# Attention and two feed-forward layers on one core: new costs and ranks in the planner that orders all work, and two small jobs moved to GpSimd

## The chip, the cores and the metric

The kernel runs on 1 core of a Trainium2 chip. The metric is device time in microseconds (us) of one execution; the time before is the median of 3 runs, 767.08 us (765.8 to 771.89).

## The reference

Three stages follow each other. Everything is float32 (the weights of the two feed-forward layers arrive as float64 words and are decoded on the chip).

- Attention: 16 heads (2 batches of 8), 768 positions, 64 channels. Six sign bits per position (q or k times a 64x6 matrix, compared with 0) give a bucket number; a query sees only keys of its own bucket. Scores are scaled by 1/8, softmax has a guard of 1e-9 in its sum, and the result is multiplied with v.
- First layer on 1536 tokens: `h = (x @ w1) * (x @ w2)`, then `h @ w3 @ w_out` (512 to 1024 to 1024 to 512 channels).
- Second layer: `silu(x @ w_gate) * (x @ w_val) @ w_out` (512 to 1536 to 512 channels).

## The kernel before

**Arithmetic.** Most float32 products are split into a rounded high part and a low part, and one product is three matmuls (`split_mm`, L284 to L286: high by high, high by low, low by high).

**Attention.** A tile `s` is 128 queries of one head against all 768 keys; there are 96 tiles, six per head. Each tile passes: scores `S{s}` on TensorE (L626, L627); `clip{s}` on VectorE, which copies the scores with a floor and takes their maximum; `nm{s}` on VectorE (the maximum times -0.125); `exp{s}` on ScalarE (L646), which also gives the row sums; six transposes `T{s}` on TensorE (L655); the two evacuations of those, `h1_{s}` on ScalarE (L659, high part) and `h2_{s}` on VectorE (low part). Two tiles make a group: `av{n}a` and `av{n}b` on TensorE (L724, L725), `ev{n}` on ScalarE (L734, L735), then `add`, `mul` and `xlo` on GpSimd. After a head's last tile its row sums get the guard and the reciprocal (`rs{hh}` on VectorE) and go to all partitions through two transfers (`so`, `si`).

**Loading a head.** `head(hh)` for heads 2 to 15 loads raw q and k (`ldraw`, SyncE's queue), loads them once more with rounding (`cast1`, two transfers issued by GpSimd, tile `KQ`, since the source is float32 and the target a rounded type), copies parts of `KQ` on the chip (`cast2` and `cast3`, SyncE's queue, tiles `KH` and `QL`), subtracts for the low parts (`lok`, `loq`, on VectorE or GpSimd), computes the bucket bits (`proj` on TensorE, `bits` on VectorE) and moves 12 rows of bits (`rows`, SyncE's queue, L569). Only then can the first score tile of the head run. There are two sets of head buffers, so a head's loads wait for the last score tile of the head before the previous one.

**Weights.** A `piece` of weights (128x512) is loaded by SyncE's queue, decoded in four steps (`e`: exponent and leading bits, `l`: next bits, on ScalarE; `s`: sign word; `b`: the bits put together on VectorE) and split in a high part `h` and a low part `r`. Step `s` may run on ScalarE or GpSimd, whichever the planner picks, and so may `e`. 24 pieces (w3, w_out) serve the product `WP` of these two matrices, whose 192 matmuls fill TensorE between attention tiles; 16 pieces (w1, w2) serve the first layer for 512 tokens ("f" products, while attention ends); 36 pieces serve the second layer for these tokens ("m" and "acc"). From about 458 us on the other 1024 tokens run through both layers with fewer products (`pair(1, ...)`, `pair(2, ...)`); the set of inputs of `pair(1, ...)`, tiles `X1...`, is prepared by `xset` before.

**The planner.** All this is written as operations with alternatives (engine and assumed cost), inputs, resources and a rank (`prio`, lower goes first). `Plan.run` steps a clock: on each engine that is free it starts the ready operation of lowest rank. The order it finds is the order in which instructions are issued; on the chip each engine and each queue goes through its own list in that order and waits in front of an instruction whose input is late. For a transfer the planner assumes a single channel (`dma_free`), a time in it (`xfer`), 0.65 and 0.9 us around it and an extra `wait`; `queue` is how many us the channel may be booked ahead for an operation to start (`Q_LOAD` for weights and v, `Q_HEAD` for heads). An operation that may not run on GpSimd and VectorE together declares a `port`; GpSimd operations of that kind wait for the VectorE ones before them.

The ranks before, as far as they matter: heads `P_HEAD` -2.6; `nm` and `rs` -1 plus 0.001 per tile; decoding and splitting of w1 and w2 `P_DF` -1, of the second layer's weights and the layers' own evacuations `P_DEC` -1; `X1` preparation `P_T` -1; evacuations `P_EV` -0.9; products with v and their evacuation `P_AV` -0.5; `exp` 0; `clip` `P_CLIP` 0.2; w3 and w_out `P_DW` 0.45. On TensorE a product of `WP` number m ranks as tile `W_FROM` + `W_STEP` m. `W_GATE` and `F_GATE` place weight loads behind score tiles, and `N_GATE` holds the `X1` preparation back until the loads of that stage of the second layer have landed.

Of the kernel before, what the change touches and what calls it, by code (L numbers as in the profile page):

```python
# [15 lines left out]
ALU = mybir.AluOpType  # L16
# [14 lines left out]
N_R, N_SUM = 1, 2  # L31
N_DEC_MOE, N_SA_MOE, N_OT = 1, 0, 2
N_ST = 5
P_OUT, P_SPLIT, P_T, P_X2, N_GATE = -3, -2, -1, -2, 4
N_WARM = 20
W_GATE, F_GATE = (2, 1), (24, 0.8)
Q_LOAD, Q_HEAD = 6, 8
P_TPE = -1
X_W, WP_W = 3, 4
PEN = 0.05  # L40
S_POOL = 0
P_DEC, P_DW, P_DF = -1, 0.45, -1
P_CLIP, P_EV, P_AV, P_HEAD = 0.2, -0.9, -0.5, -2.6
W_FROM, W_STEP = 24, 0.75
LO_ALT, LO_FAST = 1, 4
MARGIN = (2, 0)


# [1 line left out]
BOTH = ("POOL", "DVE")  # L50
# [6 lines left out]
class Plan:  # L57
# [1 line left out]


    LAT = {
        ("PE", "PE"): 0.0, ("PE", "ACT"): 0.2, ("PE", "DVE"): 0.2, ("ACT", "PE"): 0.32, ("DVE", "PE"): 0.31,
        ("POOL", "PE"): 0.31, ("SP", "PE"): 0.3, ("DVE", "POOL"): 0.2, ("ACT", "POOL"): 0.17, ("POOL", "DVE"): 0.08,
        ("POOL", "ACT"): 0.1,
    }
# [5 lines left out]
    def op(self, name, alts, deps=(), prio=0.0, acq=(), rel=(), wait=0.0, xfer=0.0, after=(), queue=1e9, port=("POOL",)):  # L71
        o = Op()
        o.name, o.alts, o.deps, o.prio, o.acq, o.rel = name, alts, [d for d in deps if d is not None], prio, acq, rel
        o.seq, o.users, o.seen, o.end, o.wait, o.xfer = len(self.ops), [], [], None, wait, xfer
        o.after = [d for d in after if d is not None]
        o.nexts, o.queue, o.port = [], queue, port
        self.ops.append(o)
        return o
# [109 lines left out]
def moe_after_bucket_attention(ctx: ExitStack, tc: tile.TileContext, qk, vv, pp, cst, w12, w3t, w_out, wgv, wo2, out):  # L188
    nc = tc.nc
    PE, ACT, DVE, POOL, SP = nc.tensor, nc.scalar, Kept(nc.vector), Kept(nc.gpsimd), nc.sync  # L190
# [34 lines left out]
    env = {}  # L225
# [73 lines left out]
    op = plan.op  # L299
# [174 lines left out]
    def head(hh):  # L474
        i = hh % 2
        a, q, k = KQ[i], QL[i], KH[i]
        before = sc.get(6 * (hh - 1) - 1)
# [94 lines left out]
        if hh < 2:  # L572
            z = 0.3 * hh
            l1 = op(f"first{hh}k", [("SP", 1.1, load_part(1))], [], -22 + hh, xfer=1.0, acq=[("W", 1)])
            o0 = o1 = op(f"first{hh}q", [("SP", 1.1, load_part(0))], [], -21.5 + hh, xfer=1.0, acq=[("W", 1)])
            r1 = op(f"round{hh}k", [("ACT", c_act(S), lambda: round_part(1))], [l1], pr_ - 3 + z)
            c3 = [("POOL", c_pool_mul(S), copy3(POOL)), ("ACT", c_act(S), copy3(ACT))]
            oc = op(f"cast3_{hh}", c3[hh : hh + 1], [l1], pr_ - (1 if hh else 6) + z)
            r0 = op(f"round{hh}q", [("ACT", c_act(S), lambda: round_part(0))], [o0], pr_ - 2.5 + z)
            o2 = op(f"cast2_{hh}", [("ACT", c_act(S), copy2)], [r1], pr_ - 2 + 2 * z)  # L580
            o3 = op(f"lok{hh}", [("DVE", c_dve(S), lo_k(DVE))], [r1, oc], pr_ + z, rel=[("W", 1)], port=BOTH)
            o4 = op(f"loq{hh}", [("DVE", c_dve(S), lo_q(DVE))], [r0, o3], pr_ - 1 + z, rel=[("W", 1)], port=BOTH)
        else:
            o0 = op(f"ldraw{hh}", [("SP", 1.1, load)], [before], pr_ - 2, acq=[("raw", 1)], xfer=1.4, queue=Q_HEAD)
            ok = o1 = op(f"cast1_{hh}", [("POOL", 2.35, cast1)], [before], pr_ - 2, xfer=2.8, queue=Q_HEAD, wait=1.0, port=())
            o2 = op(f"cast2_{hh}", [("SP", 0.48, cast2)], [before, ok], pr_ - 2, xfer=0.75, after=[o1])
            oc = op(f"cast3_{hh}", [("SP", 0.48, cast3)], [before, o1], pr_ - 2.1, xfer=0.75, after=[o1])
            o3 = op(f"lok{hh}", lo_alts(lo_k), [o0, ok], pr_, port=BOTH)
            o4 = op(f"loq{hh}", lo_alts(lo_q), [o0, o1, o3], pr_, rel=[("raw", 1)], port=BOTH)
# [27 lines left out]
    def tile_ops(s):  # L617
        hh, qt = divmod(s, 6)
        i, n, kk = hh % 2, s // 2, s % 2
        a, q, k = KQ[i], QL[i], KH[i]  # L620
        qs = slice(qt * 128, qt * 128 + 128)

        def scores():
            ps = two(f"S{s}")
            for c0, c1 in ((0, 512), (512, S)):
                PE.matmul(ps[:, c0:c1], a[:, 0, qs], a[:, 1, c0:c1], start=True, stop=False)  # L626
                PE.matmul(ps[:, c0:c1], q[:, qs], k[:, c0:c1], start=False, stop=True)  # L627

        def clip():
            env[f"ms{s}"] = ap.tile([128, S], F32, tag="ms", name=f"ms{s}", bufs=N_MS)  # L630
            env[f"mx{s}"] = ap.tile([128, 2], F32, tag="mx", name=f"mx{s}", bufs=6)
            ps = end_two(f"S{s}")
            DVE.tensor_scalar(
                out=env[f"ms{s}"], in0=ps[:, 0:S], scalar1=-BIG, scalar2=None, op0=ALU.max, op1=ALU.max,
                accum_out=env[f"mx{s}"][:, 0:1],
            )

        def negmax():
            m = env[f"mx{s}"]
            DVE.tensor_scalar(out=m[:, 1:2], in0=m[:, 0:1], scalar1=-0.125, scalar2=None, op0=ALU.mult)  # L640

        def expo():
            m, p = env.pop(f"mx{s}"), env[f"ms{s}"]
            if qt == 0:
                env[f"sums{hh}"] = ap.tile([128, 6], F32, tag="sums", name=f"sums{hh}", bufs=N_SUM)
            ACT.activation(p, p, AF.Exp, bias=m[:, 1:2], scale=0.125, accum_out=env[f"sums{hh}"][:, qt : qt + 1])  # L646

        def open_p():
            if kk == 0:
                env[f"P{n}"] = ap.tile([128, 2, 12, 128], F32R, tag="P", name=f"P{n}", bufs=N_PT)  # L650

        def pe_transp():
            ps, p = two(f"T{s}"), env.pop(f"ms{s}")
            for c in range(6):
                PE.transpose(ps[:, c * 128 : c * 128 + 128], p[:, c * 128 : c * 128 + 128], ident)  # L655

        def pe_first():
            open_p()
            ACT.copy(env[f"P{n}"][:, kk, 0:6], env[f"T{s}"][:, 0:S].rearrange("p (c q) -> p c q", c=6))  # L659

        def pe_second():
            v = end_two(f"T{s}")[:, 0:S].rearrange("p (c q) -> p c q", c=6)
            p = env[f"P{n}"][:, kk]
            sub(DVE, p[:, 6:12], v, f(p[:, 0:6]))

        pr_ = P_ATT + s * 0.001
        deps = [sc.get(s - 1), lo_op.get(s - N_MS - 1)]
        if qt == 0:
            deps += head_ready[hh]
        sc[s] = op(f"S{s}", [("PE", c_pe(4, 384), scores)], deps, pr_, acq=[("two", 1)])  # L670
        o1 = op(f"clip{s}", [("DVE", c_dve(S) + 0.12, clip)], [sc[s], clip_prev[0]], pr_ + P_CLIP, acq=[("ms", 1)], rel=[("two", 1)])
        clip_prev[0] = o1
        o2 = op(f"nm{s}", [("DVE", 0.07, negmax)], [o1], pr_ - 1)
        o3 = op(f"exp{s}", [("ACT", 0.93, expo)], [o2, exp_op.get(s - 1)], pr_, acq=[("sums", 1)] if qt == 0 else [])
        acq_p = [("PT", 1)] if kk == 0 else []
        opened = p_open.get(n)
        o6 = op(f"T{s}", [("PE", 0.58, pe_transp)], [o3, setup_ld], pr_ + P_TPE, acq=[("two", 1)], rel=[("ms", 1)])
        lo_op[s] = o6
        o6 = op(f"h1_{s}", [("ACT", c_act(S) - 0.08, pe_first)], [o6], pr_ + P_EV, acq=acq_p, after=[opened])
        p_open[n] = o6  # L680
        t_op[s] = op(f"h2_{s}", [("DVE", c_dve(S), pe_second)], [o6], pr_ + P_EV, rel=[("two", 1)])
        exp_op[s] = o3
        if qt == 5:
            rowsums(hh, o3, pr_)

    def rowsums(hh, last, pr_):

        e = hh % 2

        def recip():  # L690
            sm = env[f"sums{hh}"]
            DVE.tensor_scalar(out=sm, in0=sm, scalar1=1e-9, scalar2=None, op0=ALU.add)
            DVE.reciprocal(sm, sm)

        def put():
            env[f"rd{hh}"] = dpool.tile([128, 6], F32, name=f"rd{hh}")
            SP.dma_start(out=env[f"rd{hh}"], in_=env.pop(f"sums{hh}"))

        def get():
            if e == 0:  # L700
                env[f"R{hh // 2}"] = ap.tile([128, S], F32, tag="R", name=f"R{hh // 2}", bufs=N_R)
            row = env.pop(f"rd{hh}").rearrange("p c -> (p c)").partition_broadcast(64)
            SP.dma_start(out=env[f"R{hh // 2}"][64 * e : 64 * e + 64], in_=row)

        o1 = op(f"rs{hh}", [("DVE", 0.31, recip)], [last], pr_ - 1, port=BOTH)
        o2 = op(f"so{hh}", [("SP", 0.55, put)], [o1], pr_ - 3, xfer=0.05, wait=0.4, rel=[("sums", 1)])
        r_op[hh] = op(f"si{hh}", [("SP", 0.55, get)], [o2], pr_ - 3, xfer=0.15, wait=0.4, acq=[("R", 1)] if e == 0 else [])

# [976 lines left out]
```

## Time and profile before

| | before |
|---|---|
| median of 3 runs | 767.08 us |
| the profiled execution | 766.29 us, its span 764.5 us |
| TensorE busy | 742.8 us (97%) |
| VectorE busy | 541.1 us (71%) |
| ScalarE busy | 463.5 us (61%) |
| GpSimd busy | 320.5 us (42%) |
| TensorE clock granted | full speed in all 40 slices |
| DMA, 16 engines | 50.4% (hardware queues), 6.5% (software queue) |

The span runs from the first to the last instruction. Busy time is the union of an engine's instructions; a matmul's end is modelled, so consecutive matmuls overlap in the record (one is shown with 0.39 us where the next begins 0.23 us later). "Idle before <- releaser" names what ended the pause in front of an instruction.

### The profile page before, as it was taken

The page shows a single profiled execution, that of the slowest core. Times are in us where ns is not written, and L with a number is a line of the kernel's source. Part 1 is how long each engine was busy: PE and PEld are TensorE (multiplying, and loading weights), DVE is VectorE, ACT ScalarE, POOL GpSimd, SP SyncE. Part 2 cuts the span into 40 slices and gives each one's busy share as a digit, 9 for nine tenths or more (in the row PEclk, how much of TensorE's full clock was granted, in tenths as well). Part 3 has the DMA queues.
Part 4 walks back from the last instruction along what each step waited for, and adds up shares of the span by engine and source line. Part 5 has one row for each costly group of instructions (what it writes and reads, how often), then busy time and mean ns, then how long its engine had stood idle before and what let it go on. Part 6 is the DMA issues. An engine that isn't in the chain of part 4 may idle for free.

```text
span 764.5 us, 11354 instructions
## 1 busy us (share of the span) xinstructions
PE 742.8 (97%) x3888; PEld 627.1 (82%) x3888; DVE 541.1 (71%) x957; ACT 463.5 (61%) x835; POOL 320.5 (42%) x338
## 2 busy tenths in 40 slices
PE   8989999999999989999999999999999999999997
PEld 5867798888999868888788888888888888888886
DVE  7879897888878878556798555667676774555550
ACT  6979988999878979786897753212244322331200
POOL 3566758576545746534311234523401645330000
PEclk9999999999999999999999999999999999999999
DMA  8875566665569794599877975221225433455011
GB/s 268 216 184 140 132 170 155 163 161 135 143 153 256 218 280 150 173 353 350 286 276 281 364 269 202 101 84 55 83 73 165 139 120 110 165 167 191 28 56 55
DMA packets 43329, 135.10 MB, mean 177 GB/s; under 512 B 7893, under 2 KB 10069, under 8 KB 43273
## 3 DMA queue, kind: packets, MB, share of 16 engines
q1 hardware_dynamic: 41032, 123.38, 50.4%
q0 software_dynamic: 2240, 11.01, 6.5%
q8 instruction: 31, 0.51, 0.3%
q14 instruction: 26, 0.20, 0.1%
HBM read 97.85 MB, written 30.46 MB: 168 GB/s over the span
## 4 chain that ended last, share of the span: by engine, by line
PE 77%; DMA 8%; ACT 6%; POOL 3%; DVE 3%; issue 2%; SPq 0%; POOLq 0%; ACTq 0%; DVEq 0%
DMA KQ<-in_qk_dram 5%; PE T L655 4%; PE pacc_two L286 3%; PE pacc_two L284 3%; PE pacc_two L285 3%; PE m L284 3%; PE av L724 3%; PE m L285 3%; PE m L286 3%; PE av L725 3%; PE a L284 2%; PE a L286 2%; PE a L285 2%; PE c L286 2%; PE c L284 2%
## 5 line engine op out<-in xcount | busy, mean ns | idle before, releaser
L181 DVE TENSOR_SCALAR_CACHE_REDUCE ms<-S 128x768 f32<-128x768 f32 x96 | 91.4, 952 | 21.8 <-PE S L627 15.7
L181 DVE TENSOR_TENSOR P<-T,P 128x768 fp32r<-128x768 f32 x96 | 90.5, 952 | 10.2 <-ACT P L659 9.4
L646 ACT ACTIVATE ms<-ms,mx 128x768 f32<-128x768 f32 x96 | 89.8, 936 | 10.8 <-DVE mx L181 10.1
L655 PE MATMUL T<-cs,ms 128*128 128x128 f32 x576 | 78.3, 273 | 7.0 <-ACT ms L646 3.1
L659 ACT CAST P<-T 128x768 fp32r<-128x768 f32 x96 | 75.5, 794 | 9.3 <-PE T L655 6.2
L655 PEld LDWEIGHTS T<-cs,ms 128*128 128x128 f32 x576 | 65.4, 140 | 14.3 <-ACT ms L646 5.5
L724 PE MATMUL av<-P,VP 128*128 128x256 f32 x288 | 74.2, 292 | 0.9 <-ACT tt L735 0.7
L725 PE MATMUL av<-P,VP 128*128 128x256 f32 x288 | 71.5, 283 | 0.7 <-DVE P L181 0.7
L626 PE MATMUL S<-KQ 128*128 128x512 f32 x192 | 67.2, 353 | 4.2 <-DVE ms L181 2.1
L627 PE MATMUL S<-KH,QL 128*128 128x512 f32 x192 | 60.7, 339 | 2.2 <-DMA KH<-QL 1.5
L724 PEld LDWEIGHTS av<-P,VP 128*128 128x128 f32 x288 | 54.6, 190 | 3.3 <-ACT tt L735 2.8
L725 PEld LDWEIGHTS av<-P,VP 128*128 128x128 f32 x288 | 54.8, 190 | 1.3 <-DVE P L181 0.9
L626 PEld LDWEIGHTS S<-KQ 128*128 128x128 f32 x192 | 36.2, 188 | 13.2 <-DVE ms L181 3.7
L1392 ACT COPY u<-a 128x512 f32<-128x512 f32 x20 | 11.7, 587 | 55.5 <-PE a L286 55.4
L181 POOL TENSOR_TENSOR sl_F<-sl_F 128x256 f32<-128x256 f32 x30 | 22.2, 738 | 53.0 <-DVE sl_F L181 41.6
L627 PEld LDWEIGHTS S<-KH,QL 128*128 128x128 f32 x192 | 36.2, 189 | 8.7 <-DMA KH<-QL 1.6
L290 ACT ACTIVATE dec_w2x<-sl_raww2x 128x512 f16<-128x512 f32 (+1 forms) x54 | 39.0, 734 | 2.8 <-DVE sl_raww2x L181 2.1
L284 PE MATMUL m<-sl_X,sl_w2x 128*128 128x512 f32 x96 | 37.5, 391 | 1.0 <-ACT sa_m L937 1.0
L286 PE MATMUL m<-sl_X,sl_w2x 128*128 128x512 f32 x96 | 37.4, 390 | 0.0
L285 PE MATMUL m<-sl_X,sl_w2x 128*128 128x512 f32 x96 | 37.4, 390 | 0.0
L181 POOL TENSOR_TENSOR KQ<-kqraw,KQ 64x768 fp32r<-64x768 f32 x11 | 20.3, 1849 | 27.4 <-DVE ms L181 8.1
L181 DVE SCALAR_TENSOR_TENSOR sl_raww2x<-dec_w2x,dec_w2x 128x512 uint32<-128x512 uint32 x36 | 25.8, 721 | 7.7 <-ACT dec_w2x L290 5.4
(302 smaller groups left out, 2194.9 us busy)
## 6 DMA issues: line engine op xcount, KB each, us to landing
dram<-sl_w2x SPq DMA_DIRECT2D x36, 512.0 KB
sl_raww2x<-in_wgv_dram SPq DMA_DIRECT2D x24, 512.0 KB
KQ<-in_qk_dram POOLq DMA_DIRECT2D x28, 384.0 KB, 6.1
sl_wA<-dram SPq DMA_DIRECT2D x20, 512.0 KB
sl_wB<-dram SPq DMA_DIRECT2D x20, 512.0 KB
sl_raww<-in_w3t_dram SPq DMA_DIRECT2D x16, 512.0 KB
sl_raww12f<-in_w_dram SPq DMA_DIRECT2D x16, 512.0 KB
dram<-sl_w12f SPq DMA_DIRECT2D x16, 512.0 KB
```

Of the source, the lines that this page charges most:

```text
L181: self.got.append(call(*a, **k))
L284: PE.matmul(ps, a_hi, b_hi, start=first, stop=False, skip_group_check=more)
L285: PE.matmul(ps, a_hi, b_lo, start=False, stop=False, skip_group_check=more)
L286: PE.matmul(ps, a_lo, b_hi, start=False, stop=last, skip_group_check=more)
L290: ACT.activation(out_, in_, AF.Copy, scale=by)
L626: PE.matmul(ps[:, c0:c1], a[:, 0, qs], a[:, 1, c0:c1], start=True, stop=False)
L627: PE.matmul(ps[:, c0:c1], q[:, qs], k[:, c0:c1], start=False, stop=True)
L646: ACT.activation(p, p, AF.Exp, bias=m[:, 1:2], scale=0.125, accum_out=env[f"sums{hh}"][:, qt : qt + 1])
L655: PE.transpose(ps[:, c * 128 : c * 128 + 128], p[:, c * 128 : c * 128 + 128], ident)
L659: ACT.copy(env[f"P{n}"][:, kk, 0:6], env[f"T{s}"][:, 0:S].rearrange("p (c q) -> p c q", c=6))
L724: PE.matmul(ps[:, 0:256], vab, p[:, :, c], start=c == 0, stop=False)
L725: PE.matmul(ps[:, 0:256], vab, p[:, :, 6 + c], start=False, stop=c == 5)
```

## The change

It edits constants of the planner, two of its latencies, the assumed cost of the rounding load, and the row sums' code. The rounding load is taken to occupy GpSimd for 1.12 us instead of 2.35 and to be usable 4.2 us after the modelled transfer instead of 1.0. Evacuations rank at -2.6 instead of -0.9, heads at -4.5 instead of -2.6, `clip` at 0.7 instead of 0.2. Sign words list GpSimd before ScalarE (`S_POOL`). Heads 2 to 4 list GpSimd before VectorE for their subtractions (`LO_FAST` from 4 to 1). The guard of the row sums becomes an operation of its own on GpSimd, and only the reciprocal stays on VectorE. The two latencies into TensorE grow from 0.32 and 0.31 to 0.37 and 0.36.

```diff
-P_OUT, P_SPLIT, P_T, P_X2, N_GATE = -3, -2, -1, -2, 4
+P_OUT, P_SPLIT, P_T, P_X2, N_GATE = -3, -2, 1, -2, 6
-W_GATE, F_GATE = (2, 1), (24, 0.8)
-Q_LOAD, Q_HEAD = 6, 8
+W_GATE, F_GATE = (2, 2), (37, 1.8)
+Q_LOAD, Q_HEAD = 8, 5
-S_POOL = 0
-P_DEC, P_DW, P_DF = -1, 0.45, -1
-P_CLIP, P_EV, P_AV, P_HEAD = 0.2, -0.9, -0.5, -2.6
-W_FROM, W_STEP = 24, 0.75
-LO_ALT, LO_FAST = 1, 4
+S_POOL = 1
+P_DEC, P_DW, P_DF = -1.5, 2.15, -0.7
+P_CLIP, P_EV, P_AV, P_HEAD = 0.7, -2.6, -0.65, -4.5
+W_FROM, W_STEP = 10, 1
+LO_ALT, LO_FAST = 1, 1
+CAST_WAIT = 3
...
-        ("PE", "PE"): 0.0, ("PE", "ACT"): 0.2, ("PE", "DVE"): 0.2, ("ACT", "PE"): 0.32, ("DVE", "PE"): 0.31,
+        ("PE", "PE"): 0.0, ("PE", "ACT"): 0.2, ("PE", "DVE"): 0.2, ("ACT", "PE"): 0.37, ("DVE", "PE"): 0.36,
...
-            ok = o1 = op(f"cast1_{hh}", [("POOL", 2.35, cast1)], [before], pr_ - 2, xfer=2.8, queue=Q_HEAD, wait=1.0, port=())
+            ok = o1 = op(f"cast1_{hh}", [("POOL", 1.12, cast1)], [before], pr_ - 2, xfer=2.8, queue=Q_HEAD, wait=CAST_WAIT + 1.2, port=())
...
-        o2 = op(f"nm{s}", [("DVE", 0.07, negmax)], [o1], pr_ - 1)
+        o2 = op(f"nm{s}", [("DVE", 0.07, negmax)], [o1], pr_ - 1, port=())
...
+        def guard():
+            sm = env[f"sums{hh}"]
+            POOL.tensor_scalar(out=sm, in0=sm, scalar1=1e-9, scalar2=1.0, op0=ALU.add, op1=ALU.mult)
+
         def recip():
-            sm = env[f"sums{hh}"]
-            DVE.tensor_scalar(out=sm, in0=sm, scalar1=1e-9, scalar2=None, op0=ALU.add)
-            DVE.reciprocal(sm, sm)
+            DVE.reciprocal(env[f"sums{hh}"], env[f"sums{hh}"])
...
-        o1 = op(f"rs{hh}", [("DVE", 0.31, recip)], [last], pr_ - 1, port=BOTH)
+        last = op(f"rp{hh}", [("POOL", 0.15, guard)], [last], pr_ - 1)
+        o1 = op(f"rs{hh}", [("DVE", 0.14, recip)], [last], pr_ - 1, port=())
```

## Rows read from the trace of the kernel before

**Rows 1.** Windows over the whole span: length, busy us (count) by engine, clock, DMA share, GB/s

```profile
0.00:20.00 20.00, 15.86 (x65) 11.69 (x66) 15.40 (x32) 14.10 (x22) 7.32 (x13) 1.00 0.88 270
20.00:100.00 80.00, 72.07 (x494) 62.65 (x493) 69.07 (x139) 73.24 (x142) 52.90 (x58) 1.00 0.70 169
100.00:260.00 160.00, 159.62 (x1047) 142.60 (x1046) 133.41 (x262) 140.88 (x267) 101.15 (x105) 1.00 0.67 172
260.00:320.00 60.00, 55.69 (x359) 47.68 (x357) 47.02 (x87) 51.77 (x99) 32.98 (x37) 1.00 0.59 187
320.00:380.00 60.00, 58.87 (x259) 48.10 (x258) 36.61 (x54) 45.27 (x75) 26.23 (x29) 1.00 0.91 326
380.00:760.00 380.00, 380.00 (x1674) 314.15 (x1673) 238.84 (x387) 137.68 (x234) 99.93 (x96) 1.00 0.43 149
760.00:764.50 4.50, 0.65 (x3) 0.19 (x2) 0.71 (x2) 0.59 (x1) 0.00 (x0) 0.96 0.61 233
```

**Rows 2.** TensorE's timeline: four of its longest waits between 40 and 300 us

```profile
48.72 0.50 PE L627 MATMUL S<-KH,QL 128*128 128x512 f32 x1 [1.31 <-DMA KH<-QL]
58.25 0.47 PE L626 MATMUL S<-KQ 128*128 128x512 f32 x1 [0.89 <-DVE P L181]
91.76 0.84 PE L655 MATMUL T<-cs,ms 128*128 128x128 f32 x6 [1.21 <-DVE QL L181]
284.12 0.88 PE L655 MATMUL T<-cs,ms 128*128 128x128 f32 x6 [2.58 <-ACT ms L646]
```

**Rows 3.** The chain that ended last (start us, us, what): rounding loads in it

```profile
23.03 11.12 DMA KQ<-in_qk_dram
60.45 5.33 DMA KQ<-in_qk_dram
270.62 11.22 DMA KQ<-in_qk_dram
```

**Rows 4.** Tile KQ: us from the issue of its rounding loads to landing

```profile
DMA to landing us min/median/max: 4.3/6.1/11.2
```

**Rows 5.** Timeline of VectorE and ScalarE around 282 us (start, us, instruction, idle before)

```profile
281.86 0.95 DVE L181 TENSOR_TENSOR KQ<-kqraw,KQ 64x768 fp32r<-64x768 f32 x1 [3.10 <-DMA KQ<-in_qk_dram]
282.85 0.15 DVE L181 TENSOR_SCALAR mx<-mx 128x1 f32<-128x1 f32 x1
...
283.04 0.93 ACT L646 ACTIVATE ms<-ms,mx 128x768 f32<-128x768 f32 x1 [3.00 <-DVE mx L181]
```

**Rows 6.** SyncE's queue around the rounding load of head 2: weight loads of w_out

```profile
17.78 0.94 SPq L368 DMA_DIRECT2D sl_rawwo<-in_w_out_dram  x2
...
22.76 0.91 SPq L368 DMA_DIRECT2D sl_rawwo<-in_w_out_dram  x2
```

**Rows 7.** Groups by line and shape (busy us, mean ns, idle before)

```profile
L181 DVE TENSOR_TENSOR P<-T,P 128x768 fp32r<-128x768 f32 x96 | 90.5, 952 | 10.2 <-ACT P L659 9.4
...
L181 POOL TENSOR_TENSOR KQ<-kqraw,KQ 64x768 fp32r<-64x768 f32 x11 | 20.3, 1849 | 27.4 <-DVE ms L181 8.1 <-DVE mx L181 7.0 <-DMA KQ<-in_qk_dram 6.1
...
L181 POOL DMA_DIRECT2D KQ<-in_qk_dram x28 | 15.7, 560 | 2.6 <-PE S L627 2.3
...
L290 ACT ACTIVATE dec_w<-sl_raww 128x512 f16<-128x512 f32 x11 | 8.8, 796 | 0.3
...
L290 ACT ACTIVATE dec_w12f<-sl_raww12f 128x512 f16<-128x512 f32 x9 | 7.1, 791 | 0.2
...
L181 POOL TENSOR_SCALAR dec_w12f<-sl_raww12f 128x512 f16<-128x512 f32 x7 | 5.4, 778 | 5.8 <-ACT dec_w12f L382 3.4 <-DVE mx L181 2.0
```

**Rows 8.** Tile sums: the guard on VectorE (ns min/median/max, first and last start us)

```profile
L181 DVE TENSOR_SCALAR sums<-sums x16: 154/167/623, 28.6 to 315.4; 128x6 f32<-128x6 f32 x16
```

**Rows 9.** Tile sl_X1T: its last parts on VectorE (first and last start us)

```profile
L181 DVE TENSOR_TENSOR sl_X1T<-sl_XF,sl_X1T x7: 681/684/694, 392.7 to 412.6; 128x512 fp32r<-128x512 f32 x7
```

**Rows 10.** SyncE's queue: first fetch of split weights for the second half

```profile
441.57 0.42 SPq L1175 DMA_DIRECT2D sl_wA<-dram  x1
```

**Rows 11.** TensorE's timeline: first product of the second half with X1T

```profile
462.10 0.39 PE L284 MATMUL b<-sl_X1T,sl_wP 128*128 128x512 f32 x1
```

## The prediction

> **What bounds the kernel now.** I read the windows over the span first [rows 1]. TensorE is the bound: from 380 to 760 us it is busy for all 380.00 us, and its 1674 matmuls follow each other every 0.227 us (380 / 1674). From 100 to 260 it misses 0.38 us. No matmul is added or removed by the change, so it can only gain or lose where TensorE stands idle: 4.14 us from 0 to 20, 7.93 from 20 to 100, 4.31 from 260 to 320, 1.13 from 320 to 380, and 3.85 at the end (length less busy time, window by window). The first and last of these, 7.99 us, are the start with heads 0 and 1, loaded another way, and the drain of the last outputs; the edits reach neither in any way I can name. That leaves 0.38 + 7.93 + 4.31 + 1.13 = 13.75 us. A matmul behind a wait is also shown with 0.50 us where a flowing one has 0.39 [rows 2, 11], so each wait that goes returns about 0.1 us more.
>
> Next I read what ended those waits [rows 2]: a transfer of bucket rows (1.31 us), VectorE (0.89 and 1.21), ScalarE's exponential (2.58). Then the chain [rows 3]: it passes three times through the rounding load of a head, 11.12, 5.33 and 11.22 us long; the middle case of all 28 is 6.1 us, the worst 11.2 [rows 4]. The 2.58 us can be followed: VectorE stood 3.10 us in front of a subtraction whose rounding load had not landed; behind it in VectorE's list was a 0.15 us `nm`, for which ScalarE's exponential waited 3.00 us, and for that TensorE's transposes [rows 2, 5]. So a part of the idle time comes from a plan that believed loads too fast.
>
> Between 20 and 100 us the two helpers are nearly full themselves: ScalarE 73.24 and VectorE 69.07 of 80 us [rows 1]. What they have too much of there is not returned by a better order.
>
> **The change, part by part.**
>
> *The longer assumed load.* The modelled time from start to usable was 2.35 + 0.65 + 2.8 + 0.9 + 1.0 = 7.70 us and becomes 1.12 + 0.65 + 2.8 + 0.9 + 4.2 = 9.67. The 1.12 agrees with two issues of 0.560 [rows 7]. Subtractions, copies and bits of a head move back in the lists by about 2 us, and other work takes their place. Around 282 us the blocking shrinks from 3.10 to about 1.1 (3.10 - 1.97), and `nm` and `clip` go ahead of it. I take 2.1 of the 4.31 us in that window; bounds 0 and 4.31.
>
> *Loads spread out.* In SyncE's list four loads of w_out of 512 KB stand around the rounding load of head 2, two before and two beside it [rows 6]. With `W_GATE` (2, 2) load z ranks behind tile 2(z - 2) instead of z - 2, so most of these four go behind head 2's load. That load took 11.12 us; at the 6.1 of the middle case the head would be ready 5 us earlier, and the 1.31 us wait for its rows goes. What follows from it in the 7.93 us of the window I take as half, 4.0 us, since the two waits for VectorE [rows 2] and the full helpers [rows 1] belong to the other half; bounds -8 (a rival below) and 7.93. What is late next is VectorE's own list.
>
> *Restarts.* Some eight waits fewer at 0.1 us: 0.8 us; bounds 0 and 1.5.
>
> *Evacuations far ahead.* On each engine only passing matters. `P_EV` at -2.6 passes `nm`, `rs`, `P_DF` and `P_DEC`. Ahead of weight decoding this helps where attention ends; ahead of `nm` it costs: an `h2` of 0.952 us [rows 7] can now go before an `nm` that releases an exponential. It needs both ready in the same moment while the exponential has no other tile; TensorE has fillers after 100 us, so I charge -0.5 us; bounds -3 and 1.
>
> *Edits that pass nobody.* `clip` at 0.7 stays behind everything but w3, w_out (now 2.15) and the `X1` parts (now 1), as before with 0.2 against 0.45; the `X1` parts only went from ahead of it to behind it, and exist after attention alone. The `port` of `nm` concerns GpSimd, where `nm` cannot run. `W_FROM` 10 and `W_STEP` 1 let a `WP` product of three matmuls (0.68 us) go before a score tile earlier; TensorE's sum stays, so 0, bounds -1 and 1. The latencies grow by 0.05 us: 0.
>
> *Sign words and guard on GpSimd.* ScalarE has 11 + 9 sign words of w3, w1 and w2 at 0.796 and 0.791 us; on GpSimd one takes 0.778 [rows 7]. At most 15.9 us leave ScalarE during attention, mostly from stretches where TensorE is full, so 0 now. The guard takes VectorE 0.154 us at best and 0.623 at worst [rows 8]; on GpSimd it adds a hand-over per head in a path that only `mul` waits for, much later: 0. Bounds for both together -3.6 (a rival below) and 1.1, the idle time between 320 and 380.
>
> *`LO_FAST`.* A subtraction takes 1.849 us on GpSimd [rows 7], and 0.95 on VectorE for as many columns. If one of the heads 2 to 4 changes sides, its chain grows by 2 x 0.9 = 1.8 us; I charge -0.3; bounds -4 and 0.
>
> *`Q_LOAD` 8, `Q_HEAD` 5.* Weights may be booked 2 us further ahead and heads 3 us less. The trace shows no booking. Bounds: nothing, or 3 us per head on the heads in the first 100 us. I take nothing, since the gates thin out the weights in just that stretch.
>
> *`X1` later.* `N_GATE` 6 instead of 4 is two stages of 36 matmuls later, 2 x 36 x 0.227 = 16.3 us. The last `X1` part starts at 412.6, the fetch queued behind all of them at 441.57, the first use is at 462.10 [rows 9, 10, 11]. 412.6 + 16.3 = 428.9 is 12.7 us before the fetch: 0.
>
> Sum: -2.1 - 4.0 - 0.8 + 0.5 + 0.3 = -6.1 us. From the profiled execution, 766.29 us (span 764.5 and 1.8 around it), that is **760.2 us**. The profiled run lies 0.79 us below the median of 767.08, so against the median it is -0.9%.
>
> **A rule against it.** The guard on VectorE took up to 0.623 us where the best was 0.154 [rows 8], with the same 128x6 elements; something held it. In the Trainium skill, "SBUF — State Buffer", section "SBUF: two separate sides", VectorE and GpSimd share a port pair under an exclusive lock, and the loser is blocked for the winner's whole instruction. By that rule more elementwise work on GpSimd blocks VectorE; what it would give here is the third rival, and by it the sum would be -2.5 us instead of -6.1.
>
> **The rivals.**
>
> *All of it returns.* The new order has no late load in it: 13.75 us and 1 us of restarts, 766.29 - 14.75 = 751.5. For it: much of the idle time hangs on loads [rows 2, 3]. Against it: ScalarE and VectorE are nearly full from 20 to 100 [rows 1].
>
> *Waits change places.* A head needs the load (6.1), two subtractions (0.95 to 1.85 each), bits and the rows' transfer; a plan that counts on late loads starts these later, and as much appears elsewhere: 764 to 769. For it: the same 96 tiles and full helpers. Against it: the 3.10 us of VectorE [rows 5] have no need to return.
>
> *The port.* 20 sign words at 0.778 us are 15.6 us of GpSimd; if each holds a VectorE instruction for half of it, 7.8 us, and TensorE sees this in 140 of 300 us (20 to 100, 260 to 320), 3.6 us are lost: 760.2 + 3.6 = 763.8. For it: the 0.623 [rows 8]. Against it: the middle case is 0.167 there.
>
> *Heads too late, slower.* Heads may start only with 5 us booked, weights with 8, subtractions stand 2 us later and on GpSimd. If each of the four heads 2 to 5 comes 2 to 3 us later, at a time without ready fillers, TensorE waits 8 to 12 us more and nothing of the gain comes: 774 to 778, about 775. It decides in the first 100 us: from the point where the first score tile of head 2 starts later than before, with idle time over 7.93. For it: the head's chain is what waits there already [rows 3]. Against it: the thinned weight loads.
>
> **How the numbers follow.** The forecast (756 to 763) has 0.38, all returned 0.18 (749 to 756), waits in other places 0.21, the port 0.09, heads too late 0.14. Over 1% faster is below 759.4 us, over 1% slower above 774.8; 1% is what a measurement of this kernel can surely tell from nothing. Faster: 0.18 and half of the forecast, 0.37. Slower: most of the last, 0.11. Within: 0.52. The range of 8 in 10 leaves out the lower third of the second case (0.06) and the last case above 773 (0.13): 751 to 773. The likeliest case alone is 756 to 763.
>
> **What would show it.** Right: idle time of TensorE from 20 to 100 near 4 us and from 260 to 320 near 2, no wait of VectorE for `KQ` over 1.5 us, head 2's rounding load near 6 us, still nothing missing after 380. Wrong: a wait on TensorE at the first `b` product, which would make the `X1` step late; exponentials waiting longer for `nm` in total, which would make the evacuations' step the costly one; GpSimd as the releaser of subtractions and bits, for the head rival; VectorE's decoding instructions longer on average, for the port.

## The result, and the profile after

The changed kernel takes **760.3 us** (median of 4 runs, 759.45 to 760.82) against 768.15 for the kernel before, now with 4 runs (765.8 to 771.89): ratio 0.9887, 95% interval [0.9845, 0.9930]. The forecast was 760.2. The profiled execution took 759.9 us with a span of 758.1, so 6.4 us of span went. Lines of the code moved by 1 (up to about L690), behind that by 3 or 4.

The first view is the page's busy time by engine. TensorE lost 2.0 us and ScalarE 9.2; GpSimd gained 11.7.

```profile
PE 740.8 (98%) x3888; PEld 626.9 (83%) x3888; DVE 539.7 (71%) x944; ACT 454.3 (60%) x820; POOL 332.2 (44%) x366
```

The windows over the span, with the columns of [rows 1]:

```profile
0.00:20.00 20.00, 15.31 (x62) 11.19 (x63) 15.12 (x33) 13.80 (x21) 7.98 (x14) 1.00 0.74 221
20.00:100.00 80.00, 73.25 (x491) 63.36 (x492) 68.96 (x133) 73.49 (x142) 57.77 (x69) 1.00 0.77 200
100.00:260.00 160.00, 159.24 (x1045) 141.83 (x1044) 137.31 (x261) 137.41 (x261) 98.97 (x117) 1.00 0.68 172
260.00:320.00 60.00, 59.31 (x386) 52.77 (x385) 45.42 (x84) 50.61 (x96) 39.49 (x45) 1.00 0.66 198
320.00:380.00 60.00, 59.89 (x263) 48.91 (x262) 38.48 (x55) 46.04 (x75) 28.92 (x30) 1.00 0.93 334
380.00:755.00 375.00, 373.77 (x1648) 308.84 (x1646) 234.37 (x382) 132.93 (x229) 99.08 (x95) 1.00 0.42 147
755.00:758.10 3.10, 0.00 (x0) 0.00 (x0) 0.00 (x0) 0.00 (x0) 0.00 (x0) 0.77 0.36 137
```

Length less busy time gives TensorE's idle time, window by window against [rows 1]: 4.14 became 4.69 at the start, 7.93 became 6.75 from 20 to 100, 0.38 became 0.76 from 100 to 260, **4.31 became 0.69 from 260 to 320**, 1.13 became 0.11 from 320 to 380, and 3.85 became 4.33 behind that (the last two rows). The sum is -4.4 us, with -2.0 of busy time -6.4.

TensorE's timeline, its longest waits after 40 us and the place that answers to the 2.58 us of [rows 2]. The wait for head 2's rows grew from 1.31 to 2.14 us, but it ends earlier (46.96 us instead of 48.72); the 2.58 is now 0.46:

```profile
46.96 0.47 PE L628 MATMUL S<-KH,QL 128*128 128x512 f32 x1 [2.14 <-DMA KH<-QL]
56.41 0.85 PE L656 MATMUL T<-cs,ms 128*128 128x128 f32 x6 [0.88 <-ACT P L660]
81.68 0.50 PE L286 MATMUL wps<-sl_wo,sl_w 128*128 128x512 f32 x1 [0.96 <-POOL sl_wo L182]
227.48 0.36 PE L728 MATMUL av<-P,VP 128*128 128x256 f32 x1 [0.67 <-POOL QL L182]
281.29 0.85 PE L656 MATMUL T<-cs,ms 128*128 128x128 f32 x6 [0.46 <-DVE ms L182]
```

GpSimd's group that answers to the second row of [rows 7]: it stood idle 27.4 us in front of these subtractions and now stands 1.1.

```profile
L182 POOL TENSOR_TENSOR KQ<-kqraw,KQ 64x768 fp32r<-64x768 f32 x10 | 18.4, 1844 | 1.1 <-POOL sl_w L182 0.4
```

Tile `KQ`, as in [rows 4]. This row now counts six on-chip copies too (`QL<-KQ`, `KH<-KQ`); the 28 loads alone took 4.1 to 9.0 us with 6.1 in the middle, so they are no faster there, and only the 11 us cases are gone.

```profile
DMA to landing us min/median/max: 2.6/5.8/9.0
```

### The profile page after: what moved, and what is told of

Read it like the earlier page. It is cut to its first block, busy times and chain, and to the rows that moved or that the text cites. A ratio compares the mean times of both kernels' runs of the same rounds, so it can differ in the third digit from the quotient of the medians.

```text
span 758.1 us, 11357 instructions
## 1 busy us (share of the span) xinstructions
PE 740.8 (98%) x3888; PEld 626.9 (83%) x3888; DVE 539.7 (71%) x944; ACT 454.3 (60%) x820; POOL 332.2 (44%) x366
## 4 chain that ended last, share of the span: by engine, by line
PE 72%; DVE 1%; issue 1%; ACT 1%; POOL 0%; DVEq 0%; ACTq 0%; POOLq 0%
PE T L656 4%; PE m L285 3%; PE pacc_two L286 3%; PE pacc_two L285 3%; PE pacc_two L287 3%; PE m L287 3%; PE m L286 3%; PE d L287 2%; PE c L287 2%; PE a L287 2%; PE a L286 2%; PE d L286 2%; PE c L286 2%; PE d L285 2%; PE c L285 2%; PE a L285 2%
## 5 line engine op out<-in xcount | busy, mean ns | idle before, releaser
L182 DVE TENSOR_TENSOR P<-T,P 128x768 fp32r<-128x768 f32 x96 | 90.8, 954 | 13.5 <-ACT P L660 12.3
L647 ACT ACTIVATE ms<-ms,mx 128x768 f32<-128x768 f32 x96 | 89.9, 937 | 11.9 <-DVE mx L182 11.2
L182 POOL TENSOR_SCALAR dec_w2x<-sl_raww2x 128x512 f32<-128x512 f32 (+1 forms) x23 | 16.9, 734 | 49.2 <-DVE sl_w2x L182 14.9
L291 ACT ACTIVATE dec_w2x<-sl_raww2x 128x512 f16<-128x512 f32 (+1 forms) x49 | 34.6, 730 | 1.4 <-DVE sl_raww2x L182 1.0
```

The costliest lines, as they stand in the source:

```text
L182: self.got.append(call(*a, **k))
L291: ACT.activation(out_, in_, AF.Copy, scale=by)
```

## The experiments

Each edit below changes a few of the planner's numbers, so the whole order is found anew, except in "order frozen". "Waits" is the sum of all waits of 0.15 us or more that the timeline shows in front of TensorE's instructions, some 4 us of which lie in the first 20 us in every kernel. "Loads" is GpSimd's idle time in front of its subtractions `KQ<-kqraw`, all in us. [rows 7] names VectorE as what ended most of it, but before the two longest, 8.08 and 7.00 us, the load had landed only 0.23 and 0.22 us earlier, so it is time in front of loads. "Profiled" is the execution whose trace was read; one trace for each kernel. Each ratio is to runs of the kernel before on the same chip (medians 767.8 to 768.8), as recorded; it is not the quotient of the two medians.

| kernel | median | ratio to before [95%] | profiled | waits | of them 100 to 260 | of them 260 to 320 | loads |
|---|---|---|---|---|---|---|---|
| before | 768.15 | 1 | 766.29 | 17.2 | 0.4 | 4.2 | 27.4 |
| after | 760.3 | 0.9887 [0.9845, 0.9930] | 759.9 | 12.6 | 0.7 | 0.7 | 1.1 |
| wait of head 15 | 766.66 | 0.9985 [0.9956, 1.0014] | 765.67 | 16.8 | 1.7 | 2.6 | 28.6 |
| load alone | 760.95 | 0.9916 [0.9883, 0.9949] | 759.84 | 12.3 | 1.7 | 0.0 | 0.8 |
| gate alone | 767.43 | 0.9998 [0.9977, 1.0019] | 767.19 | 18.2 | 1.5 | 2.9 | 22.7 |
| latencies alone | 762.55 | 0.9928 [0.9901, 0.9955] | 761.53 | 15.2 | 1.6 | 0.4 | 20.9 |
| issue cost alone | 766.07 | 0.9976 [0.9957, 0.9995] | 767.18 | 17.1 | 2.7 | 0.8 | 27.1 |
| after, old load | 764.48 | 0.9959 [0.9937, 0.9980] | 764.11 | 14.1 | 1.8 | 0.4 | 12.9 |
| after, old ranks | 766.89 | 0.9972 [0.9951, 0.9994] | 767.47 | 19.1 | 4.7 | 0.6 | 0.5 |
| after, old GpSimd work | 771.44 | 1.0039 [1.0018, 1.0060] | 769.08 | 19.1 | 4.0 | 1.7 | 0.7 |
| order frozen | 765.28 | 0.9956 [0.9936, 0.9976] | 766.21 | 14.7 | 2.4 | 0.3 | 0.8 |
| after, old latencies | 769.57 | 1.0012 [0.9995, 1.0028] | 768.97 | 19.9 | 8.1 | 0.3 | 2.3 |
| after, head 2 earlier | 767.72 | 0.9994 [0.9969, 1.0019] | 766.38 | 16.7 | 5.7 | 0.2 | 6.1 |
| load and latencies | 770.82 | 1.0033 [1.0013, 1.0053] | 769.54 | 19.7 | 6.0 | 0.9 | 3.8 |

Four parts were first put on the kernel before, each alone.

**Wait of head 15.** Only the load behind the 3.10 us of [rows 5] is assumed later.

```diff
-wait=1.0
+wait=1.0 + 4.0 * (hh == 15)
```

> The kernel before, with 4 us more assumed wait for the rounding load of head 15 alone; all lists are the same up to about 270 us. Theory (a plan that believes the load too fast blocks VectorE in front of nm): the 3.10 us wait of VectorE for KQ and the 2.58 us wait of TensorE at 284 us go; idle time of TensorE from 260 to 320 falls from 4.31 to about 2 us; time 2 to 2.5 us shorter (ratio about 0.997). Rival (the waits only change places): idle time there stays between 3.5 and 5 us, ratio 0.999 to 1.001.

766.66 us: the interval holds the 2 us expected as well as nothing. VectorE's 3.10 us and the 2.58 on TensorE are gone, and TensorE's idle time from 260 to 320 fell from 4.31 to 2.62 us; it has new waits at the same head, a few us on:

```profile
289.38 0.45 PE L545 MATMUL proj<-KQ,pst 128*108 128x512 f32 x1 [1.11 <-issue]
290.42 0.48 PE L546 MATMUL proj<-QL,pst 128*108 128x512 f32 x1 [0.59 <-DMA QL<-KQ]
```

The head's chain was still late, so a part of the wait moved to its next link. The lists of this kernel and of the kernel before are the same up to 278 us, yet the traces show 1.7 and 0.4 us of waits from 100 to 260: differences of that size in the column are scatter between executions.

**Load alone.** The whole rounding-load edit, all heads.

```diff
-[("POOL", 2.35, cast1)] ... wait=1.0
+[("POOL", 1.12, cast1)] ... wait=4.2
```

> The kernel before with the rounding load's new assumed cost and wait (1.12 us and 4.2 us) and nothing else. Theory (the longer assumed load is the step that pays where attention ends): idle time of TensorE from 260 to 320 near 2 us, time 2 to 4 us shorter than before, no wait of VectorE for KQ over 1.5 us. Rival (gain comes from the ranks and from GpSimd's share): less than 1 us shorter, or longer.

760.95 us: this edit alone gives as much as the whole change. TensorE has no wait of 0.15 us left between 260 and 380 us, and GpSimd no longer stands in front of its subtractions (whether the second explains the first, the next runs show):

```profile
L181 POOL TENSOR_TENSOR KQ<-kqraw,KQ 64x768 fp32r<-64x768 f32 x10 | 18.5, 1848 | 0.8
```

**Gate alone.**

```diff
-W_GATE, F_GATE = (2, 1), (24, 0.8)
+W_GATE, F_GATE = (2, 2), (24, 0.8)
```

> The kernel before with W_GATE (2, 2) alone, so that w_out's loads stand behind head 2's. Theory of the prediction: the rounding load of head 2 lands after about 6 us instead of 11, the rows' wait of 1.31 us goes, idle time from 20 to 100 falls from 7.93 to about 4 us, time 4 us shorter. Rival (the load lands earlier, but the lists put its readers where they were): the load lands earlier, idle time from 20 to 100 stays within 1 us of 7.93, time within 1 us of before.

767.43 us, ratio 0.9998: nothing. The load did come sooner (its first reader runs at 27.81 us instead of 32.09, head 2's first scores at 42.4 instead of 47.0), and the wait for its rows is gone. TensorE's timeline shows what took its place, one head later:

```profile
57.14 0.76 PE L546 MATMUL proj<-QL,pst 128*108 128x512 f32 x1 [2.91 <-POOL QL L181]
```

**Latencies alone.** The step that I had costed at nothing.

```diff
-("ACT", "PE"): 0.32, ("DVE", "PE"): 0.31
+("ACT", "PE"): 0.37, ("DVE", "PE"): 0.36
```

> The kernel before with the two latencies into TensorE 0.05 us longer and nothing else; by itself this changes no instruction's cost, but the planner finds another order from the first microseconds on. Theory (named waits decide): within 2 us of before. Rival (any new order moves the time by as much as this whole change did, so 6 us can be a lucky order): more than 3 us away from before in either direction.

762.55 us, ratio 0.9928: an assumption moved by 0.05 us gives most of the gain of the load edit, although GpSimd still stands 20.9 us in front of late loads. TensorE's waits from 260 to 320 us are gone here too (0.4 left).

Then parts of the load edit, and single parts taken out of the changed kernel.

**Issue cost alone** (on before): the smaller occupation of GpSimd without the longer wait.

```diff
-[("POOL", 2.35, cast1)]
+[("POOL", 1.12, cast1)]
```

> The kernel before with the rounding load's assumed issue cost at 1.12 us instead of 2.35 and its wait left at 1.0, so the planner believes the load 1.23 us earlier than before and finds another order. Theory (belief in the load decides): engines stand in front of late loads at least as long as before (VectorE and GpSimd together over 25 us in front of the two subtractions), time 767 to 772 us. Rival (any new order is better than the one before): 760 to 764 us.

766.07 us, between the two forecasts, and 27.1 us in front of the loads: the longer `wait`, not the cheaper issue, takes the standing away. But in the window from 260 to 320 us TensorE misses only 1.02 us, although GpSimd stands 3.82 us in front of head 15's load there. That subtraction was VectorE's in the kernel before, with an `nm` behind it [rows 5]; here it is GpSimd's. The window, columns of [rows 1]:

```profile
260.00:320.00 60.00, 58.98 (x386) 51.81 (x385) 48.19 (x98) 53.15 (x101) 36.01 (x38) 1.00 0.60 187
```

GpSimd's timeline:

```profile
280.15 1.84 POOL L181 TENSOR_TENSOR KQ<-kqraw,KQ 64x768 fp32r<-64x768 f32 x1 [3.82 <-DMA KQ<-in_qk_dram]
```

**After, old load.**

```diff
-[("POOL", 1.12, cast1)] ... wait=CAST_WAIT + 1.2
+[("POOL", 2.35, cast1)] ... wait=1.0
```

> The changed kernel with the rounding load's old cost and wait (2.35 and 1.0 us), all other edits kept. Theory: the engines stand in front of rounding loads again, TensorE loses 3 to 6 us, time 763 to 767 us. Rival (the other edits carry the gain): within 1 us of the changed kernel's 760.3.

764.48 us: without this edit about a third of the gain is left (0.41 of 1.13%), and GpSimd stands 12.9 us in front of loads again, with 0.4 us of TensorE's waits from 260 to 320.

**After, old ranks.**

```diff
-P_DEC, P_DW, P_DF = -1.5, 2.15, -0.7
-P_CLIP, P_EV, P_AV, P_HEAD = 0.7, -2.6, -0.65, -4.5
+P_DEC, P_DW, P_DF = -1, 0.45, -1
+P_CLIP, P_EV, P_AV, P_HEAD = 0.2, -0.9, -0.5, -2.6
```

> The changed kernel with all seven ranks of its two lines back to their old values (evacuations at -0.9). Theory (the longer assumed load is enough): within 2 us of 760.3. Rival (evacuations far ahead pay where attention ends): 763 us or more, with idle time of TensorE from 240 to 320 over 3 us.

766.89 us. Of the 6.5 us of new waits, 4.0 lie between 100 and 260 us (4.7 against 0.7), where the kernel before lost 0.38, 2.0 before 100, and 0.4 at the end of attention.

**After, old GpSimd work.**

```diff
-S_POOL = 1
+S_POOL = 0
...
-        def guard():
-            POOL.tensor_scalar(...)
         def recip():
+            DVE.tensor_scalar(...)
             DVE.reciprocal(...)
```

> The changed kernel with sign words on ScalarE first and the guard on VectorE again. Theory: within 2 us of 760.3, ScalarE's busy time about 8 us longer. Rival (ScalarE's relief pays in the first 260 us): 763 us or more. Rival (the shared port costs time, so that taking work off GpSimd pays): 758 us or less, with VectorE's decoding instructions shorter on average.

771.44 us, slower than before and 9 us outside what the theory allowed. But the order was found anew, so this is no price of the words; the next run is.

**Order frozen.** The sign words that the planner gives to GpSimd (30) keep their place in the plan and are issued by ScalarE instead; the instruction lists of TensorE, VectorE and SyncE are those of the changed kernel.

```diff
-("POOL", c_pool_mul(512), sign(POOL))
+("POOL", c_pool_mul(512), sign(ACT))
```

> The changed kernel with the lists of TensorE, VectorE and SyncE's queue exactly as they are; the 30 sign words that the planner gave to GpSimd are issued by ScalarE at the same place in the program (20 of them for w3, w_out, w1 and w2). This prices ScalarE's load without a new order. Theory (the 8 sign words that the change moves are worth little; it is the order that counts): 30 sign words cost less than 3 us, time 760 to 763 us. Rival (ScalarE's relief is what the old setting lost in the reversal of GpSimd's share): 764 to 772 us, TensorE waiting for ScalarE. Rival (the shared port): VectorE's decoding instructions shorter on average and 758 us or less.

765.28 us: 30 words cost 5.0 us on ScalarE, 0.17 each, more than the 3 us I had allowed. The change moved only 8 words (GpSimd had 22 before), so an estimate from this row is 8 x 0.17 = 1.3 us of its gain.

**After, old latencies.** The edit of "latencies alone", taken back.

> The changed kernel with the two latencies into TensorE 0.05 us shorter, as before; no instruction costs another time, only the order differs. Theory (the changed settings are good as settings): within 2 us of 760.3. Rival (they are good only in this exact order): 763 to 770 us, TensorE waiting more in total than the 12.6 us of the changed kernel, in places that have nothing in common with those of before.

769.57 us: 9.3 us for 0.05 us of assumption, most of it as waits from 100 to 260 us (8.1 against 0.7).

**After, head 2 earlier.** The plan believes head 2's load, alone, 3.2 us sooner.

```diff
-wait=CAST_WAIT + 1.2
+wait=CAST_WAIT + 1.2 - 3.2 * (hh == 2)
```

> The changed kernel with 3.2 us less assumed wait for the rounding load of head 2 alone, whose load landed early there but whose subtraction started no earlier than before (34.37 us in both). Theory (the 5 us that the load gained were given back by the plan): the subtraction starts by 32 us, the bits' product of head 2 by 37.5, the wait of TensorE for head 2's rows (2.14 us) shrinks below 1; time 759 to 761 if the rest of the order is as good. Rival (new order, new waits): 763 us or more.

767.72 us. The subtraction runs at 29.59 us instead of 34.37 and the 2.14 us wait is gone, as expected; but 5 us of new waits appear from 100 to 260, and the time is the rival's.

**Load and latencies** (on before): the two edits that gave 0.8% and 0.7% alone.

> The kernel before with two edits that were each alone 5 to 8 us faster: the rounding load's new cost and wait, and the latencies. If they stand for separate losses they add up: 754 to 757 us. If both only replace the same unlucky stretch around 282 us by another order: 760 to 765 us.

770.82 us, ratio 1.0033 [1.0013, 1.0053]. Both forecasts missed: together they make the kernel a little slower than it was. Two of the waits in TensorE's timeline:

```profile
177.01 0.87 PE L655 MATMUL T<-cs,ms 128*128 128x128 f32 x6 [1.39 <-ACT ms L646]
180.59 0.58 PE L724 MATMUL av<-P,VP 128*128 128x256 f32 x1 [2.71 <-ACT tt L735]
```

## Why the prediction was right, and where it was not

The number held (760.2 against 760.3), but that was luck: three of its terms were off, two too small (260 to 380 us, restarts) and one too large (20 to 100), and 1.4 us of idle time came in windows where I had put nothing (0.55 at the start, 0.38 from 100 to 260, 0.48 at the end).

**The longer assumed load: right where VectorE stood, and one way out of several.** -2.1 us forecast for 260 to 320, -3.6 measured, and another -1.0 from 320 to 380 where I had put nothing. "Load alone" shows that the edit suffices: the standing in front of loads falls from 27.4 to 0.8 us and TensorE's waits from 260 to 380 vanish. But GpSimd's standing is not what TensorE waited for: "latencies alone", "issue cost alone" and "after, old load" keep the old `wait`, GpSimd stands 12.9 to 27.1 us in them, and 0.4 to 0.8 us of waits are left from 260 to 320. Their orders gave head 15's subtraction to GpSimd. VectorE stands in front of that load in two kernels only, 3.10 us before and 2.13 in "gate alone", and these two lose most in the window, 4.2 and 2.9 us. "Wait of head 15" agrees in part: the blocked pair of [rows 5] went, but with it only 1.7 of the 4.31 us.

**Loads spread out: the step that failed.** -4.0 forecast from 20 to 100, -1.2 measured, and 0.9998 for the gate alone. The transfer did what I said: head 2's load took 6.1 us instead of 11.12. In the changed kernel SyncE's queue has these loads of weights around it:

```profile
18.09 0.47 SPq L369 DMA_DIRECT2D sl_rawwo<-in_w_out_dram  x1
...
21.04 0.43 SPq L369 DMA_DIRECT2D sl_raww<-in_w3t_dram  x1
...
28.23 1.35 SPq L369 DMA_DIRECT2D sl_rawwo<-in_w_out_dram  x1
29.69 0.50 SPq L516 DMA_DIRECT2D QL<-KQ  x1
...
42.39 0.80 SPq L570 DMA_DIRECT2D KH<-QL  x1
```

One load of w_out instead of two, twice, and one of w3 between them; the first reader of `KQ` runs at 29.69 us instead of 32.09. What I left out is that the subtraction behind it has a place in GpSimd's list, and that list believes the load late. GpSimd's timeline:

```profile
23.08 1.27 POOL L182 DMA_DIRECT2D KQ<-in_qk_dram  x2 [0.72 <-PE S L628]
...
31.59 0.67 POOL L182 TENSOR_SCALAR dec_wo<-sl_rawwo 128x512 f32<-128x512 f32 x1 [1.69 <-DVE sl_rawwo L182]
32.22 0.67 POOL L182 TENSOR_SCALAR sl_wo<-sl_rawwo 128x512 fp32r<-128x512 f32 x1
32.97 1.32 POOL L182 TENSOR_TENSOR sl_wo<-sl_rawwo,sl_wo 128x512 fp32r<-128x512 f32 x1
34.37 1.83 POOL L182 TENSOR_TENSOR KQ<-kqraw,KQ 64x768 fp32r<-64x768 f32 x1
```

The half that this subtraction reads landed at 29.93 us, instead of 34.15; the subtraction starts at 34.37, behind decoding of w_out. It had started at 34.37 before as well, after 7.00 us of standing. So the time that GpSimd stood there is now used for weights, and head 2's rows are issued no earlier, at 42.39 us instead of 41.54. They landed 4.4 us after that instead of 7.1, which the prediction had not counted on, and TensorE began head 2's first score tile at 44.34 instead of 47.01, so that it waits longer for rows that come earlier. This is the rival "waits change places", true from 20 to 100 us; "heads too late" is not borne out (first score tile earlier, idle time 6.75). My test for the step was a rounding load near 6 us, which came true and proved nothing about the head.

**Restarts:** busy time fell by 2.0 us where 0.8 was forecast; this miss, too, went into the number that held. Ends of matmuls are modelled, so I don't divide it further.

**Latencies and "edits that pass nobody": wrong as a way of counting.** On the kernel before, `P_CLIP` with `P_DW`, `P_AV` alone and `F_GATE` alone leave every engine's list as it was, as argued. `W_FROM` with `W_STEP`, `LO_FAST`, and `Q_LOAD` with `Q_HEAD` each give other lists from the loading of heads 2 to 4 on; no run times them alone, so the 0.3 us charged for `LO_FAST` and the 0 for the others stay unmeasured. The 0.05 us leave the lists alone up to 51 us on the kernel before and 84 us on the changed one (not "from the first microseconds", as I expected), reorder what follows, and are worth -0.72% on the kernel before, 9.3 us in the changed one, and +10 us on top of the load edit (760.95 to 770.82).

**Evacuations:** ScalarE's exponentials waited 10.1 us in total for `nm` before and 11.2 now (the row: us in all, times, longest). That is 1.1 us more where 0.5 was charged, within the bound of 3, and it is ScalarE's idle time, not TensorE's. "After, old ranks" loses 6.6 us, but with a new order, so no run prices this step.

```profile
ACT ms L647 <- DVE mx L182: 11.2, 13, 2.3
```

**Sign words and guard: 0 forecast.** 8 words moved, 3 of them among the 20 that I had counted on, since GpSimd was their helper already; about 1.3 us by "order frozen". The guard on GpSimd (tile `sums`, columns of [rows 8]) takes no less than on VectorE:

```profile
L182 POOL TENSOR_SCALAR sums<-sums x16: 196/201/708, 27.4 to 307.0; 128x6 f32<-128x6 f32 x16
```

**The port** is not borne out. In "order frozen", with 30 words fewer on GpSimd, VectorE's steps `b` take 720, 763, 746 and 695 ns on average in the four weight groups (second layer, w3, w1 with w2, w_out), against 706, 752, 820 and 690 in the changed kernel: no shorter in three of four. Against the kernel before (721, 818, 749, 768) the change made them shorter in three of four, though GpSimd's busy time grew. The rule cited from the Trainium skill, "SBUF — State Buffer", section "SBUF: two separate sides", is not seen in this row. That does not refute it: the planner's `port` plans such instructions of the two engines apart and makes GpSimd's wait for VectorE's, and no run takes that away.

**`X1` later: right, 0.** The last part starts 14.4 us later than in [rows 9], 16.3 were worked out; the fetch is at 434.26 us, and no matmul waits after 380.

```profile
L182 DVE TENSOR_TENSOR sl_X1T<-sl_XF,sl_X1T x7: 684/686/731, 408.7 to 427.0; 128x512 fp32r<-128x512 f32 x7
```

**What the runs show together.** A longer assumed load does one thing reliably: engines stop standing in front of loads (0.5 to 6.1 us in all seven kernels planned with it, the frozen one included, besides the changed one; 12.9 to 28.6 in the others). The time doesn't follow that column: 760.3 to 771.44 us with it, 762.55 to 767.43 in the five edited kernels without. It follows TensorE's waits, all of which lie before 380 us, but roughly: the best two have 12.3 and 12.6 us of them, those with 19 to 20 took 766.89 to 771.44, and between them the order is not kept (14.1 and 14.7 us took longer than 15.2). So the 1.1% belongs to this set of numbers as a whole. It was shown that the load edit alone is enough for it on the kernel before, and that it is undone by 0.05 us of another assumption. **What makes one order better than another from 100 to 260 us, where these kernels lose between 0.4 and 8.1 us, stays open**; no run here names a single cause.

## What to carry to other kernels

When a planner writes the order, a longer assumed latency moves the reader back in a list: it frees the engine that stood there, but it doesn't make the datum's user any earlier, so count the user's place in the list before booking a faster transfer as gain. Ask what stands behind a blocked instruction, too: 3.10 us of VectorE in front of a load cost TensorE 2.58, since an `nm` stood behind it, while 3.82 of GpSimd stood in a window that missed 1.02 in all. Price an edit of costs or ranks by the new order, not by its size, and judge it from several plans that differ by little, since here 0.05 us decided over 9 us in either direction. To price moved work, freeze the order and let another engine issue it.

## What the runs showed of the hardware

TensorE's granted clock fell after a wait in the traces of six of the twelve edited kernels. In "gate alone" the 2.91 us wait at 57 us is followed by a stretch at half speed (1.2 instead of 2.4 GHz); the windows of that kernel, columns of [rows 1]:

```profile
56.00:58.00 2.00, 0.86 (x2) 0.73 (x3) 1.64 (x1) 0.61 (x3) 2.00 (x3) 0.72 0.09 33
58.00:60.00 2.00, 2.00 (x11) 1.87 (x9) 0.99 (x1) 0.34 (x1) 1.99 (x4) 0.50 0.90 224
60.00:62.00 2.00, 2.00 (x18) 2.00 (x17) 1.78 (x4) 1.72 (x4) 1.48 (x2) 0.93 1.15 222
```

A group of six transposes there took 1.48 us instead of 0.85. "Load and latencies" has such a stretch behind its 2.71 us wait, "after, old GpSimd work" behind one of 2.47, "issue cost alone" behind one of 2.12, "order frozen" behind one of 1.58 at 20.82 us, and "after, head 2 earlier" behind three of 1.61, 1.06 and 0.61 close together, while the 2.58 of [rows 2] and the 2.14 of the changed kernel left the clock at 1.00. The length of the wait alone doesn't tell it, and a few us of waiting can cost more than they show as waiting.

It also differs between executions of one kernel. Of 83 runs of the kernel before on three chips, the 26 with a mean granted clock of 1.000 have a median of 766.65 us, the 33 with 0.998 one of 768.55; every run of the changed kernel and of "load alone" shows 0.999 or 1.000. The trace of the kernel before is from a run at 1.000. So the medians lie 7.85 us apart and the two profiled runs only 6.4; that the clock makes this difference of 1.5 us is an estimate from these rows.
